# Two cached attention blocks on one core: the Q projection in matmuls of 320 columns instead of 160, with smaller first weight loads, no second warm-up and a new order table

## The chip, the cores and the metric

The kernel runs on one core of a Trainium2 chip. The metric is the device time of one execution in microseconds (us), as the median of three runs; lower is better. Before the change it is 734.2 us (runs 734.12, 734.2 and 735.46).

## The reference, cut to what matters

Two independent problems, A and B, with their own inputs; their outputs are put side by side. For each of them, with 16 batch rows (`B`), 80 query positions (`Sq`), model width 576 (`D`), 32 query heads, 16 key/value heads, 512 cached positions (`Sk`) and head width 128 (`Dh`), all in bfloat16:

```python
q = (x @ wq).reshape(B, Sq, 32, 128).transpose(0, 2, 1, 3)   # x: 16 x 80 x 576, wq: 576 x 4096
k = repeat(k_cache, 2, axis=1)                               # k_cache, v_cache: 16 x 16 x 512 x 128
v = repeat(v_cache, 2, axis=1)
scores = einsum("bhqd,bhkd->bhqk", q, k) * 128 ** -0.5
o = einsum("bhqk,bhkd->bhqd", softmax(scores), v)
out = o.transpose(0, 2, 1, 3).reshape(B, Sq, 4096) @ wo      # wo: 4096 x 576
```

## The kernel before

**Tiling.** The work is cut into 128 units. A unit is one batch row with four key/value heads, that is eight query heads, or 640 rows of scores against 512 cached positions. Eight units (eight batch rows, the same eight heads) make an octet; there are 16 octets, and two octets run interleaved, unit by unit. The constants are `NG` octets, `goct` the octet's number, `bl` the batch row inside it, and `U` the unit's number.

**One unit on TensorE (PE).** Scores come as four matmuls of 128 rows (`qk`, line 684) and one tile for the 32 rows that each head pair has left over (`qkr`, line 671, which packs four small matmuls into strips of the array, for two units at a time). VectorE (DVE) takes the negated row maximum (line 693), ScalarE (ACT) the exponential with its row sum (line 697), DVE the reciprocal (line 703), and GpSimd (POOL) scales the rows (line 706). Then PE transposes the probabilities in 40 small matmuls that use the two halves of the array's rows (`tr`, line 738), DVE or ACT copy them out of PSUM (lines 749 to 758), PE multiplies with V (`pv`, line 781), and DVE or ACT copy the result to `oT` (line 795). The output projection (`op`, line 830) adds 16 heads at a time.

**The Q projection.** For each octet there are eight sessions, `m` = 0 to 7. The contraction over 576 is done as four chunks of 128 rows and a tail of 64 rows. Before the change a session covers two batch rows (160 columns of `xT`) and four heads. Each of its two halves (`qp`, line 550) puts two heads side by side into one PSUM bank, eight matmuls of 160 columns. The tail (`qt`, line 565) adds four matmuls of 64 rows, two of which share the array because they use different row halves; outside the first two octets it is emitted at the head of a unit's `tr`. Two evictions of 320 columns (`qev`, lines 578 and 579) then scale the result and write it to `qT`. A session is tied to the unit `us` at whose `tr` its tail runs; sessions with `us` under 2 come ahead of the units.

**Loads.** All loads are issued on SyncE's queue (SP), in order. K comes through transposing DMAs, one for two units (`ldk`, line 637, 1 MB each, three pairs of buffers); V as one copy for each unit (`ldv`, line 641, 512 KB, six buffers); the Q weights `wq_sb` as one copy of 1 MB for octet pairs (`ldwa`, line 514), only that of the very first octet in four pieces of 256 columns; the tail rows `wt` in two copies of 64 KB (`ldwt`, line 518); x of problem A in blocks (`ldx`, line 387, two and then three blocks of 128 rows for each half of the batch rows); `wo_sb` in four copies for each half of the heads (`ldwo`, line 606).

**Start.** PE first runs eight matmuls on zeros (`warm`, line 348), later three more (`warm2`, line 363), and transposes x of problem A (`xtr` and `xt`, lines 408 and 426).

**What sets the order.** Every operation belongs to a stream with an order of its own (a sort key). A table of letters written out by hand, `ORDER`, then merges the streams: each letter takes the next operation of its stream, a quote mark ahead of it picks the other one of DVE and ACT, and digits behind it name the PSUM banks. Each engine runs its operations in the table's order, and the waits between engines are worked out from reads and writes. So the table fixes what stands behind what on each engine and on SP.

Of the kernel before, what the change touches and what calls it, by code (L numbers as in the profile page):

```python
# [13 lines left out]
LA = 11.5  # L14
# [14 lines left out]
NWARM2 = 3  # L29
NWC = 4  # L30
RG = ((0, 1, 2), (3, 4))
TS0 = 4.5
US0 = 2
QF = 12
LQ = 11
# [3 lines left out]
Q0K = ((-6.0, 1.0, 6.0, 11.0), (-4.6, 2.5, 8.0, 13.0))  # L39
# [13 lines left out]
WQ1 = -21  # L53
# [6 lines left out]
LETTERS = "abcdefghijklmnopqrstuvwxyzABCDEFGHIJKLMN"  # L60
ORDER = """
nEJni7GJIHIHMHj3k4Hj5LLHEHad3j7Md5j6k2LKdd4A'Bj6d3Ldj5A'Bd6d3dd4Bd1dd3A'B'AJKd0LaEdd4'A'Bd5e0e1odf2'Aod3lpe7d4
lodme0Ad6'Boe1ld3BJloe2hdhCe7old4uaoe0lvd5Cole1NudAf2ld7up'Be6ouj0md3Llodf02'ABd1'Bp'Ak3j4lpd5CmLdue7Be6md4ou'
Ae0CCd5loudKvlhAg1237oaN'Be4u'wj6x'zk5oe1ule2j7LuK'yolg0356LlCof47u'xz'yc1uclpj3vd5CLme2upc6e3'w'suoe4cmd1holF
g07CouFltc2av'ycxe6B'wd3u'zse0loc7d2olce1ltg46o'Ae0le7od5'zc1Colucc6scluxd0Ct'wv'yf17A'Budpe6'Be2ud3Cpme0uoc4m
cud1A'sholg57FCoFlue4zad6'yvolf27uwc5lpcd0A'x'tpe4mg35o'Bd2C'zyve1lwc5uocme3c4suc'Aoe5ld7te6loe4b1xo'Ble3Cobul
oub5lqhCluhe0e1hoe6ug34aolbCo'xu'yClue0qd3w'Bvd5'zAoulf17g24ulppmc6cc0scc1'tzc'xe6'sd0Cwumoc4e1u'ycod7'Avltc2e
3Bclhog46hCsalue1wc5o'xe2u'ycd3z'Bv'Ae4tle7d6Coub5oluoe0lbolc4'qcf12'slg57pCe4uy'xb0'wmBhuC'zhod5uhc7Alcavpe1e
6boutle4Coe3ud7mquc1olcg02vo'slCc6uyce1x'te4uzd0'wlod6'Be2olb3olc7Cue1lbou'Ach'qf25shlg34apCpc7u'zcb1C'wC'yuA'
xmve0e4od3muc2t'Bucold5vslf67ug02pub'wz'xmpc4'Be2q'ye6oe5h'Acd1holhd3Colug02lud6y'tv'we5'zxc4Bcmc2oe0e3'sCcoau  # L70
c7'tcAle4ue2oc1lcsd5olg07tob3'x'zy'wlBe1e0oblCoulc7he2e5uhocc4v'se1qclCd7uth'Ad3Coluf06olug24Cplub5'zumve1e4'x
oab'yu'wCpluc2comud0sc1'qe6le2ocd5'Atlg47o'BCf16uw'ze3lpub7'yCAvmoe2e0ve4ob'xluoc1uC'qcle3usd7aolc1ucp'Bd2log0
5tld4z'xe1'wB'yd3Cmoe0uc5oclug26slAIf15C'zxGue7'ye0hob6v'BIoluhe2Ce3plbuo'wumd7CAv'qe0oc4lcuoc6lcutc2clpe1e4oa
d3's'tog06ld2'wz'yd1xmBc6e0lAe3cCoue7'sg45Colvoc6'zuce0'ytd5uloe6ub4hlCoIule3e7uob'xa'wlvBCd0'AqulCf16ovg24plu
c3'yzuce7mwd2xuCo'sc4'Bce1'td3olg04AhlGe7'yc5Ccx'zvpb1wumoe0e4uobluole6uc7o'qcld0tc1A'Bf47'slcpe2'sd3Comug56pl
ue1xc4'zwaco'ye2d6t'Aloc5cc4lsce0Bd5mCove1g23tluof47u'zwAe0lb3pI'xo'Bhe1mbhCou'yhpe6hluc4oe2cld5Covle0d1saulqg
46ouCe2'wxub3'yBmuoe1lc4oblzclc7e0d6'qo'Ace1'sc3oe2lcd5t'tlog07f34w'zxe1'Ab7'yolCCe0ublouplc6ve1cmoad2uCd0Clqu
sc3'Bcug67'tuf15'zxupe3'yb7u'w'BAmvoc6ce0C'sd4uhole2hvbolhuhpld3qg06Cpuc7'wzu'xd2'yAc'Be0mhe6oc3c'td4ole1sc7lC
coug03htluCe6yd7'wv'x'zAe1d0umoc3uocle2Bc5'scole6hg34Ctlauof15'wvC'Axb2zlup'Bue7e6'yobumolc3qce0ld4oe1e2Csld6v
og37upub0xmBole6e5abzlo'wc7'yCcqu'Ae1oc3le0ud4old6ole2c'tc5sclCg17ou'thf03v'ywhAe5'xu'ze1ob4lCo'Bc7lcCpvd6se2m  # L80
uc5ocld7uhte0lug15oauCle2wbuo'zuyle0d5Ad1xCC'Boue2'qg67pulob4u'w'yzlue0bomCAle2uFc7ocFve6'sd3oFluf07FCqlve5pc4
'xcupd6'tmBc2cog14'slc2ye0'x'zcwe5oe1'Ad4moc3clCBd7vtlc6ouJe0e2'scoulg35tulof16'wC'zyd0u'ACe5xlue3Bc4cpud7h'sC
oe2umJb4Joulaoe1ulbolpg35lre2w'ze4Cyc1u'xb5ovAbluComue0rcld3uoe2'Bvd5loag46le0z'tc7'xe2'ywcoc6'se1k4olcd7o'Ac0
lBcCd3Kluf25'tvhCsg14DupDc6wuhcz'Ad0mupd4'xCymug27Buf15t'x'Bc3p'ye6caoc4mcsd2'twle1e4b3'zCo'Aue7oe0lvboluod6lr
g14lphe7z'yc3Dc'wohme0c4hb1olCAlue5xcoe2u'te7ad0'sCBule4obuolvc3Colce2urc6lcoue1e7sd5log34'tColuf26C'zvb1'x'wu
'yAe4lpue0d3oDubholvc7'Brcle4d5oamg01slb7y'z'wp'Ae0c4Come1ucbltuoe2d3loe0d4rDlohe1'xg67hCBluhof25'wDu'zAc0'yCc
pue7'sc3Cd6lxvoc'Buc0mthcd4Cuplg13u'suc7z'x'we0'ycvoe2'Be3ac1'Auoe4lcoc6lctd0Cmse7vd2olug15Ctluf36z'w'xu'yb4o'
AuBle0e1hod5hc7plce2Csbmvouod7lurg03lpDe1'ze4oc2'yce3x'thb0o'walAe2Blc5obolcCre1luc7oe4d3uold2Csclue0Cg15'toum
uf47'w'yb6vpGxumCDe1pbhvlAIoue4'zId3Blue0Cod5uCrg12luoDb6'xau'Blue5bmo'ze0c7'yod4lre1colc2e6cCslud5Co'tg07u'wl
Auf12w'yxue3p'ze6c0'BCchoumd7Ac5vlocd4vh'tplDg13use5zmc6e0oc'xac3'scwye2'td6loc3e1B'Acld5oc7olcg04Ct'suClf27ux  # L90
y'Be3u'ze1we5Job0uColvbpluAe4mc3ovd6rulcod2'shpe0lJg15ohe4zmIb3DC'xCoulac7e5ulcoe0bu'to'yvBle7d4ould2rle1Cwug0
5o'AuClf37xyuc6'wc'Bpc1'zve0scmue2oc6'Acte5G'sd3ColJd4oDle1hg06olhd2I'ywzac5'x'Ae0Cpclvc3d6t'Buome1cuoe5'sc4cu
log37tulCf04ulCwb1pv'x'yB'zue5k3moe6uc7boluKlce0d5'Aoc3re2lcCoe6ud1'so'tue0lg37hoDlCb2auwz'xlue6'ye7ob'A'Bpld3
oc5me0cold6rc4cse1'tg27olf45'ywhe0'zpb2hlCDxuoe7hbCvCloud1pmd0ur'ACle4ug23oa'Bule7xb6yumuc4'wcAuc5cBbvsoe0td4l
Crd5u'zoe1ug67olvf23Dw'zyhe0lc7xDcp'Bc6'se1oc'Ae7mhoc5cd4lCoud2'tsule0pc6cvlog15tle7xd6z'yae0'wo'Be1c5mcCouc2l
cCAd3u'sC'tf47oulg25pulb0vxmBuCw'ye1e3hoe4u'zbh'Aouloc6ue2ld5ovle1crc3lscDd4oe0lg26oa'tCCb1luxp'wue3'AbmouB'yu
e0Cd5'zoue2le7od4vlrg36ulohf01ylc2xc'wCzc3u'Ac'spe7v'the6c5'BoDcumb3Coulpe0uc4loe2e7abolC'sd6urld5vcug23tob4mz
lxe0boCle1uFre7d3o'wFu'Bd4'yCDAulf05FovDg26plFuc1'yxcCwuc7mBe2co'ze4d0'tA'sd6olg37plc2w'ye1xcC'Azvc3mcoe0ud4't
aole7c3od5lse1lcoe0c2'scolg37B'tf16y'wlb2Cxp'B'Ae0Cd3'zvohme5uc7ocle4ue1obluo'se0ulqc5ad7pulcoug24Ctlud1w'zue5
e0mob4xCo'Be6ub'youle2vqlc7hcAhc4lochd3s'te0lCug45ouCCf27'wx'zyud6'Aple5uc4oe1mcud0B'soulg23pvld4y'we5'zxe1oac  # L100
2'Acmd3Covc6ltcue7Blc2oc'sg05tlCf12z'x'w'ye7e6'Aob5Colvhe0c4h'Boculc7hpe3uchlbshuomd4uple0ud6og13Ctuqb7'zyulxw
e1Ce5moauc3ce0ovle2bAuloe1'Bod4lc6Coud5lscu'qe0Clg23ovtf17ulzb6u'xw'ype0e2moe3baolBd1loc5cqd0lsCg26'Aue5u'zxb3
o'wAlc4pe6d1'yhCoucmc5Bhcule2td7o'sf04lg56pCpe2u'ybxmovd5'wC'zuBc0qle7ucoe6'the3ud2'Aolg01Coulc7xu'wcy'zc6cA'B
c1mthe0cCaod5lue2'svc4lcd3utog67slf04Czu'ye1e2xb7ouovlbp'wlBe1c6Amchoe2c3'soe0lce6od5lCd1qulog27vpb0utmCwuCyle
3e4avbo'zuxod6'Blqe1d7o'Ae0lCg35olf24wxAd1'BClye7vc6oc'zuhc3'sce0u'thc6oe5lGb3uoIlupIe7buComuclqd0ule2e3ob5'so
lg67pe2xlbwCyv'zc3Cmouce7q'Bhc6ucloae0e5uo'Ad4'tud2olusg13lCuf67xlzuc0'ycpe5'Be3od1'w't'Ad2olpg04mCuc5y'xc'zhc
# [12 lines left out]
3umCoDue0'se6hod1ulc5pvlce2obv'taClug05ruob3'zuyle0e6'x'wbCmoule2vrc7co'Bd3'soDlc5e0DAcld7og46tlCvf12w'x'yBue0
'Ae5pd4'zuomd3uog67lplc1xcCw'yc0uze5mcoud6'tse7le2oae0c1'BcCAle5uc3od4'suolcvg17tlf23x'yoe0'zb1o'BlCwe7upd4lho  # L120
# [146 lines left out]
def bass_concat_heads__gqa_block_cached__gqa_block_cached__near_ridge_kernel(  # L267
# [27 lines left out]
    with ExitStack() as es:  # L295
# [55 lines left out]
        def em_warmend(e):  # L351
# [4 lines left out]
              name="warm", stream="W", alloc=[vw])  # L356
        S.add("dve", -980, em_warmend, reads=[R(vw, 0)], writes=[R(("warm",), 1)], name="warmend", stream="warmset")
        vw2 = S.bank()

        def em_warm2(e, vw=vw2):  # L360
            last = None
            for _ in range(NWARM2):
# [580 lines left out]
```

## Time and profile before

| what | value |
|---|---|
| median of three runs | 734.2 us |
| the profiled execution's own time | 733.71 us |
| its span, from the first to the last instruction | 732.0 us |
| granted TensorE clock over the span | 1.00 |
| PE busy | 719.2 us |
| ACT busy, DVE busy | 646.7 us, 639.3 us |
| moved by DMA | 160.90 MB, mean 220 GB/s |

Times in a timeline count from the span's start. The page names an engine, a line of the kernel, the tile written and the tiles read, the shape, the count, the busy time and the mean of one. A matmul's busy time overlaps that of the next one, since they are pipelined; what one costs in a row of them is therefore read from the distance between starts. "Idle before" is time in which the engine did nothing, with what ended it behind the arrow.

### The profile page before, as it was taken

Reading aid. Unit: us, or ns where it says so; the run is one execution under the profiler, and the core shown is the slowest. Engines: PE = TensorE matmul, PEld = TensorE weight load, DVE = VectorE, ACT = ScalarE, POOL = GpSimd, SP = SyncE. Lnnn points to the kernel's source line nnn. Section 1 sums busy time; section 2 is a strip of 40 time slices with the busy share of each in tenths; the row PEclk is TensorE's granted clock in tenths of the full one; section 3 lists DMA queues with packets and bytes.
Section 4 is the critical chain, followed back from the end, with each engine's and each line's share of the span. In section 5 each row is a group of like instructions: output and inputs, shape, how many; then the busy total and the mean of one; then the engine's idle time right before and its main releaser. Section 6 shows DMA issues by size and latency. Waiting matters only on the chain.

```text
span 732.0 us, 28848 instructions
## 1 busy us (share of the span) xinstructions
PE 719.2 (98%) x12103; PEld 565.2 (77%) x12103; DVE 639.3 (87%) x1457; ACT 646.7 (88%) x1847; POOL 433.9 (59%) x650
## 2 busy tenths in 40 slices
PE   7999999999999999999999999999999999999998
PEld 5677787777877777778777877787887878777677
DVE  2988888988899888899898998989889998889995
ACT  2998889999989899999898988899989989999993
POOL 0555557654766556566556565565755746647773
DMA  9999976988989899999989999899889998699951
GB/s 253 248 231 258 285 204 175 251 201 197 261 204 258 208 233 261 229 234 268 225 215 221 234 239 215 180 240 242 223 177 241 240 225 223 130 231 216 235 134 47
DMA packets 362354, 160.90 MB, mean 220 GB/s; under 512 B 274416, under 2 KB 358640, under 8 KB 362224
## 3 DMA queue, kind: packets, MB, share of 16 engines
q1 hardware_dynamic: 362224, 159.05, 92.7%
q8 instruction: 96, 1.57, 0.9%
q14 instruction: 34, 0.28, 0.1%
HBM read 87.65 MB, written 2.95 MB: 124 GB/s over the span
## 4 chain that ended last, share of the span: by engine, by line
PE 94%; DMA 2%; ACT 1%; DVE 1%; issue 1%; SPq 0%
PE ps L830 22%; PE ps L781 19%; PE ps L550 18%; PE ps L684 15%; PE ps L738 10%; PE ps L671 5%; PE ps L565 4%; DMA kT<-in_A_k_cache_dram 2%; DMA wt<-in_A_wq_dram 1%; ACT p_sb L697 1%; DVE negmax L693 0%; ACT qT L578 0%; DVE oT L795 0%; SPq L514 0%; ACT pT L749 0%
## 5 line engine op out<-in xcount | busy, mean ns | idle before, releaser
L706 POOL TENSOR_SCALAR p_sb<-p_sb,rinv 128x512 bf16<-128x512 bf16 x640 | 432.1, 698 | 280.2 <-DVE rinv L703 279.6
L697 ACT ACTIVATE p_sb<-ps,negmax 128x512 bf16<-128x512 f32 x640 | 442.0, 706 | 28.5 <-DVE negmax L693 21.4
L693 DVE TENSOR_REDUCE negmax<-ps 128x1 f32<-128x512 f32 x640 | 419.6, 680 | 37.2 <-PE ps L684 27.1
L781 PE MATMUL ps<-pT,v_sb 128*128 128x160 bf16 x2048 | 191.0, 233 | 2.2 <-ACT pT L756 1.2
L830 PE MATMUL ps<-wo_sb,oT 128*128 128x288 bf16 x1280 | 181.4, 286 | 0.0
L550 PE MATMUL ps<-xT,wq_sb 128*128 128x160 bf16 x2048 | 178.2, 233 | 1.7 <-DMA wq_sb<-in_A_wq_dram 1.6
L781 PEld LDWEIGHTS ps<-pT,v_sb 128*128 128x128 bf16 x2048 | 152.7, 98 | 34.2 <-issue 3.5
L684 PE MATMUL ps<-kT,qT 128*128 128x512 bf16 x512 | 177.2, 380 | 0.0
L550 PEld LDWEIGHTS ps<-xT,wq_sb 128*128 128x128 bf16 x2048 | 149.4, 98 | 22.8 <-issue 2.6
L830 PEld LDWEIGHTS ps<-wo_sb,oT 128*128 128x128 bf16 x1280 | 121.1, 98 | 44.4 <-ACT pT L756 2.5
L697 ACT ACTIVATION_READ_ACCUMULATOR p_sb<-ps,negmax 128x1 f32 x640 | 140.9, 220 | 0.0
L749 ACT COPY pT<-ps 128x512 f32<-128x512 f32 x165 | 96.5, 601 | 10.5 <-PE ps L738 9.8
L738 PE MATMUL ps<-ident,p_sb 64*128 64x64 bf16 x5120 | 96.1, 190 | 2.0 <-issue 0.7
L738 PEld LDWEIGHTS ps<-ident,p_sb 64*128 64x128 bf16 x5120 | 88.0, 95 | 4.9 <-issue 1.5
L578 ACT ACTIVATE qT<-ps 128x320 bf16<-128x320 f32 x140 | 62.0, 453 | 17.8 <-PE ps L565 14.2
L795 DVE CAST oT<-ps 128x320 bf16<-128x320 f32 x132 | 63.5, 481 | 9.5 <-PE ps L781 8.4
L751 DVE COPY pT<-ps 128x1024 bf16<-128x1024 bf16 x91 | 62.1, 682 | 9.9 <-PE ps L738 8.7
L795 ACT CAST oT<-ps 128x320 bf16<-128x320 f32 x124 | 53.9, 442 | 10.4 <-PE ps L781 9.5
L684 PEld LDWEIGHTS ps<-kT,qT 128*128 128x128 bf16 x512 | 47.9, 97 | 19.0 <-ACT p_sb L697 3.8
L579 DVE TENSOR_SCALAR qT<-ps 128x320 bf16<-128x320 f32 x116 | 55.3, 481 | 6.0 <-PE ps L565 2.6
L758 DVE COPY pT<-ps 128x256 bf16<-128x256 bf16 x133 | 36.4, 282 | 10.6 <-PE ps L738 8.2
L671 PE MATMUL ps<-kT,qT 128*32 128x512 bf16 x512 | 40.0, 384 | 2.2 <-DMA kT<-in_A_k_cache_dram 1.7
(33 smaller groups left out, 196.4 us busy)
## 6 DMA issues: line engine op xcount, KB each, us to landing
v_sb<-in_A_v_cache_dram SPq DMA_DIRECT2D x64, 512.0 KB, 5.3
v_sb<-in_B_v_cache_dram SPq DMA_DIRECT2D x64, 512.0 KB, 5.0
wo_sb<-in_A_wo_dram SPq DMA_DIRECT2D x8, 576.0 KB, 6.6
wo_sb<-in_B_wo_dram SPq DMA_DIRECT2D x8, 576.0 KB, 7.0
wq_sb<-in_B_wq_dram SPq DMA_DIRECT2D x4, 1024.0 KB, 6.0
wq_sb<-in_A_wq_dram SPq DMA_DIRECT2D x3, 1024.0 KB, 6.2
out_dram<-osb SPq DMA_DIRECT2D x40, 72.0 KB, 3.8
wq_sb<-in_A_wq_dram SPq DMA_DIRECT2D x4, 256.0 KB, 5.6
```

The lines of the kernel that those rows point to most:

```text
L550: last = e.matmul(ps[:, vbq[h].phys, QO + 160 * r:QO + 160 * r + 160], lhsT=wq_sb[:, wsl, ck, hi * 128:(hi + 1) * 128], rhs=xT[:, half, ck ...
L671: last = e.matmul(ps[32 * g4:32 * g4 + 32, vb_.phys, :], lhsT=qT[:, qsl_, bl_, g4 * 160 + 128:g4 * 160 + 160], rhs=k_of(U_, g4), start=Tru ...
L684: return e.matmul(ps[:, vb.phys, :], lhsT=qT[:, qsl, bl, gl * 160:gl * 160 + 128], rhs=k_of(U, gl), start=True, stop=True)
L693: return e.tensor_reduce(negmax[:, si:si + 1], ps[:, vb.phys, :], axis=AX.X, op=AluOpType.max, negate=True)
L697: return e.activation(p_sb[:, psl, :], ps[:, vb.phys, :], AF.Exp, bias=negmax[:, si:si + 1], scale=1.0, accum_out=rowsum[:, ss, k:k + 1])
L706: return e.tensor_scalar(p_sb[:, psl, :], p_sb[:, psl, :], rinv[:, ss, k:k + 1], 1.0, op0=AluOpType.mult, op1=AluOpType.mult)
L738: last = e.matmul(dst, lhsT=p_sb[64 * h:64 * h + 64, psls[k_], j * 128:(j + 1) * 128], rhs=ident[64 * h:64 * h + 64, 64 * h:64 * h + 64], ...
L749: return e.copy(pT[:, pts, :, :].bitcast(F32)[:, :, 32 * h:32 * h + 32], ps[:, vtp[h].phys, :].rearrange("p (n c) -> p n c", n=16))
L751: return e.tensor_copy(pT[:, pts, :, 64 * h:64 * h + 64], psb[:, vtp[h].phys, :].rearrange("p (n c) -> p n c", n=16))
L781: last = e.matmul(ps[:, vo.phys, off:off + 160], lhsT=v_sb[:, vs, gl, j * 128:(j + 1) * 128], rhs=pT[:, pts, 4 * gl + j, :], start=(j == 0 ...
L795: return (e.copy if en == "act" else e.tensor_copy)(dst, src)
L830: last = e.matmul(ps[:, vb.phys, 0:DC], lhsT=oT[:, hi, rb * 128:(rb + 1) * 128], rhs=wo_sb[:, wi, c3 * DC:(c3 + 1) * DC], start=(hi == 0), ...
```

## The change

A session now covers four batch rows (320 columns) and two heads, so that a half is one head: four matmuls of 320 columns in place of eight of 160, and two tail matmuls of 320 in place of four of 160. Session 0 to 3 of an octet make batch rows 0 to 3 for all heads, 4 to 7 the others. The eviction writes four runs of 80 columns instead of two by two. Since 320 columns need three blocks of x, x is loaded three blocks first and then two. The weights of the second octet are loaded in four pieces like those of the first, each on a semaphore of its own, and the tail weights are laid out in four groups of 128 columns, not two of 256. `LQ` goes from 11 to 12, so each session belongs to a unit one earlier, and the first one of the sessions that come ahead of the units is added to them. The second warm-up is gone. `ORDER` is new throughout, with PSUM banks and the choice of DVE or ACT.

```diff
-NWARM2 = 3
-QF = 12
-LQ = 11
+LQ = 12
-Q0K = ((-6.0, 1.0, 6.0, 11.0), (-4.6, 2.5, 8.0, 13.0))
+Q0A = -6.0
+Q0B = 1.3
-WQ1 = -21
+WQ1 = -28.0
+WQ1S = 0.3
+W4 = 2
...
-        wt = sb("wt", [128, 2, 2, 256], BF16)
+        wt = sb("wt", [128, 2, 4, 128], BF16)
...
-        S.add("pe", -LA - 13.2, em_warm2, reads=[R(("ones",), 0), R(("warm",), 1)], writes=[R(vw2, 0)],
-              name="warm2", stream="X", alloc=[vw2])
...
-        XP = ((0, 2), (2, 5))
+        XP = ((0, 3), (3, 5))
...
-            pieces = () if half else [(256 * i_, 256 * i_ + 256) for i_ in range(4)] if goct == 0 else ((0, 1024),)
+            pieces = () if half else [(256 * i_, 256 * i_ + 256) for i_ in range(4)] if goct < W4 else ((0, 1024),)
...
-                    src = wq_ap[512:D, q * 1024:(q + 1) * 1024].rearrange("p (a h c) -> h p a c", a=2, h=2)
+                    src = wq_ap[512:D, q * 1024:(q + 1) * 1024].rearrange("p (a h c) -> h p a c", a=4, h=2)
...
-                bp, hq = divmod(m, 2)
-                b0 = 2 * bp
+                bq, hp = divmod(m, 4)
+                b0 = 4 * bq
...
-                        for r in range(2):
-                            hi = 4 * hq + 2 * h + r
-                            for ck in range(4):
-                                last = e.matmul(ps[:, vbq[h].phys, QO + 160 * r:QO + 160 * r + 160],
-                                                lhsT=wq_sb[:, wsl, ck, hi * 128:(hi + 1) * 128],
-                                                rhs=xT[:, half, ck, n0:n0 + 160], start=(r == 0 and ck == 0), stop=False)
+                        hi = 2 * hp + h
+                        for ck in range(4):
+                            last = e.matmul(ps[:, vbq[h].phys, QO:QO + 320],
+                                            lhsT=wq_sb[:, wsl, ck, hi * 128:(hi + 1) * 128],
+                                            rhs=xT[:, half, ck, n0:n0 + 320], start=(ck == 0), stop=False)
...
-                    for r in range(2):
-                        for h in range(2):
-                            last = e.matmul(ps[:, vbq[h].phys, QO + 160 * r:QO + 160 * r + 160],
-                                            lhsT=wt[64 * h:64 * h + 64, wsl, hq, r * 128:(r + 1) * 128],
-                                            rhs=xT[64 * h:64 * h + 64, half, 4, n0:n0 + 160],
-                                            start=False, stop=(r == 1), tile_position=(64 * h, 0))
+                    for h in range(2):
+                        last = e.matmul(ps[:, vbq[h].phys, QO:QO + 320],
+                                        lhsT=wt[64 * h:64 * h + 64, wsl, hp, :],
+                                        rhs=xT[64 * h:64 * h + 64, half, 4, n0:n0 + 320],
+                                        start=False, stop=True, tile_position=(64 * h, 0))
...
-                        c_ = (4 * hq + 2 * h) * 80
-                        dst = qT[:, qsl, b0:b0 + 2, c_:c_ + 160].rearrange("p b (r s) -> p r b s", r=2)
-                        src = ps[:, vbq[h].phys, QO:QO + 320].rearrange("p (r b s) -> p r b s", r=2, b=2)
+                        c_ = (2 * hp + h) * 80
+                        dst = qT[:, qsl, b0:b0 + 4, c_:c_ + 80]
+                        src = ps[:, vbq[h].phys, QO:QO + 320].rearrange("p (b s) -> p b s", b=4)
```

The new table also sets a new order on SP. At the start it issues both parts of x, then all weights of the first two octets in eight pieces with their tail rows, then two K loads in a row; the four copies of `wo_sb` for the first half of the heads come ahead of the K load for units 8 and 9, where two of them came behind it. On PE all four sessions that make rows 0 to 3 of the first octet and the four of the second stand ahead of the first scores.

More of the change, by code (lines that the diff above doesn't have):

```diff
@@ L58 @@
 WOL = 1.2
-LETTERS = "abcdefghijklmnopqrstuvwxyzABCDEFGHIJKLMN"
+LETTERS = "abcdefghijklmnopqrstuvwxyzABCDEFGHIJKLMNO"
 ORDER = """
[L62 to L70, printed above, removed]
@@ L320, in bass_concat_heads__gqa_block_cached__gqa_block_cached__near_ridge_kernel @@
         sem_names = (["e_pe", "e_act", "e_dve", "e_pool", "d_x00", "d_x01", "d_x10", "d_x11", "d_wo",
-                      "d_wq0", "d_wq1", "d_wqs1", "d_wqs2", "d_wqs3", "d_wt0", "d_wt1", "d_xt"]
+                      "d_wq0", "d_wq1", *["d_wqs%d%d" % (i, j) for i in range(2) for j in range(1, 4)], "d_wt0", "d_wt1", "d_xt"]
                      + ["d_out%d" % i for i in range(NOSB)]
@@ L357, in bass_concat_heads__gqa_block_cached__gqa_block_cached__near_ridge_kernel @@
         S.add("dve", -980, em_warmend, reads=[R(vw, 0)], writes=[R(("warm",), 1)], name="warmend", stream="warmset")
[L358 to L362, printed above, removed]
-                last = e.matmul(ps[:, vw.phys, :], lhsT=ones, rhs=warm, start=True, stop=True)
-            return last
-        S.add("pe", -LA - 13.2, em_warm2, reads=[R(("ones",), 0), R(("warm",), 1)], writes=[R(vw2, 0)],
-              name="warm2", stream="X", alloc=[vw2])
-        S.add("dve", -LA - 13.1, em_warmend, reads=[R(vw2, 0)], writes=[R(("warm",), 2)], name="warmend",
-              stream="warmset")
         IDENT = R(("ident",), 0)
@@ L544, in bass_concat_heads__gqa_block_cached__gqa_block_cached__near_ridge_kernel, with em_qp @@
                 for h in range(2):
[L545 removed]
+                    def em_qp(e, h=h, hp=hp, wsl=wsl, half=half, n0=n0, vbq=vbq):
                         last = None
[L547 to L553 removed]
@@ L558, in bass_concat_heads__gqa_block_cached__gqa_block_cached__near_ridge_kernel, with em_qt @@
+                        return last
+                    S.add("pe", x + 0.001 * h, em_qp, reads=[R(("wq", wsl, hp), wv)] + xr,
+                          writes=[R(vbq[h], 0)] + [R(("qT", qsl, bl, 2 * hp + h), goct) for bl in range(b0, b0 + 4)],
                           name="qp%d.%d.%d" % (goct, m, h), stream="Q",
                           alloc=[vbq[h]])
-                def em_qt(e, hq=hq, wsl=wsl, half=half, n0=n0, vbq=vbq):
+                def em_qt(e, hp=hp, wsl=wsl, half=half, n0=n0, vbq=vbq):
@@ L579, in em_qev @@
                         return e.tensor_scalar(dst, src, SCALE, None, op0=AluOpType.mult)
-                    wr_ = [R(("qT", qsl, bl, 4 * hq + r), goct) for bl in (b0, b0 + 1) for r in (2 * h, 2 * h + 1)]
+                    wr_ = [R(("qT", qsl, bl, 2 * hp + h), goct) for bl in range(b0, b0 + 4)]
                     td["q"].append((em_qev, wr_))
@@ L607, in em_ldwo @@
                                            src.rearrange("(h p) n -> p h n", p=128))
-                    S.add("sp", x, em_ldwo, writes=[R(("wo", wos), ci)] + ([R(("warm",), 3), R(("ones",), 1)] if ci == 0 else []),
+                    S.add("sp", x, em_ldwo, writes=[R(("wo", wos), ci)] + ([R(("warm",), 2), R(("ones",), 1)] if ci == 0 else []),
                           dsem="d_wo", name="ldwo%d.%d.%d" % (prob, hh, wc), stream="wo")
```

145 lines of the change are left out of this document (75 added, 70 removed).

## The prediction

> **What bounds the kernel now.** I read the page's busy times and its chain first.
>
> ```profile
> PE 719.2 (98%) x12103; PEld 565.2 (77%) x12103; DVE 639.3 (87%) x1457; ACT 646.7 (88%) x1847; POOL 433.9 (59%) x650
> ...
> PE 94%; DMA 2%; ACT 1%; DVE 1%; issue 1%; SPq 0%
> ```
>
> PE is busy for 98% of the span and makes 94% of the chain that ended last. Since a busy PE need not be PE at its pace, the view of waits, for PE alone, comes next (who waited for whom, us in total, times, longest).
>
> ```profile
> PE ps L671 <- DMA kT<-in_A_k_cache_dram: 1.7, 1, 1.7
> PE ps L550 <- DMA wq_sb<-in_A_wq_dram: 1.6, 1, 1.6
> PE ps L348 <- DVE wo_sb L341: 1.2, 1, 1.2
> PE ps L781 <- ACT pT L756: 1.2, 1, 1.2
> PE ps L781 <- issue: 0.9, 1, 0.9
> PE ps L565 <- DMA wt<-in_A_wq_dram: 0.9, 1, 0.9
> ```
>
> There is nothing longer; with four smaller rows PE waits for some 10 us of 732. The timeline of PE shows what a matmul costs in a row of them (start, us, line, shape, count):
>
> ```profile
> 62.44 0.81 PE L684 MATMUL ps<-kT,qT 128*128 128x512 bf16 x3
> 63.19 0.31 PE L565 MATMUL ps<-xT,wt 64*128 64x160 bf16 x4
> 63.34 0.75 PE L738 MATMUL ps<-ident,p_sb 64*128 64x64 bf16 x40
> 64.02 1.15 PE L830 MATMUL ps<-wo_sb,oT 128*128 128x288 bf16 x8
> 65.00 0.38 PE L684 MATMUL ps<-kT,qT 128*128 128x512 bf16 x1
> 65.22 1.27 PE L550 MATMUL ps<-xT,wq_sb 128*128 128x160 bf16 x16
> 66.42 0.61 PE L671 MATMUL ps<-kT,qT 128*32 128x512 bf16 x8
> ```
>
> Read it by starts. The eight matmuls of 288 columns take 65.00 - 64.02 = 0.98 us, 122.5 ns each; the one of 512 takes 0.22 us; four tails take 0.15 us. The sixteen of 160 take 1.20 us: 15 at 69 ns, and 165 ns for the last, because PE passes there from the whole array to a part of it, which costs 96 ns more. From all starts in the trace the medians are 69.2 ns for 160 columns, 122.5 for 288 and 216 for 512: a straight line, about 2.5 ns and 0.417 ns a column. So a Q matmul is already paid nearly by its columns.
>
> **The ledger.** Adding, over all neighbours in PE's program of before, the usual distance of such a pair of lines gives 718.0 us. PE's last matmul starts at 729.1 us, so all its waits together are 11.1 us: 3.2 by the time the first weights are there, 0.6 in small ones up to 45 us, 1.8 at K for units 8 and 9 (53 us), 1.4 at 69 us and 4.1 later, 1.7 of it near 690 us. From there to the end of the span it is 2.9 us, and I leave that alone: both programs end with the same matmuls of lines 781 and 830.
>
> **The change part by part, on PE.**
> - Main matmuls: 1024 pairs of 160 become 1024 of 320. The line gives 135.8 ns for 320, against 2 x 69.2: 2.6 ns a pair, 2.7 us. The bounds are 138.4 (two of the old ones, no gain) and 133.3 (columns alone, a gain of 5.2 us); I take the line, since 288 is its near neighbour. In the new program the array is entered from whole to row halves 135 times, not 129, at 96 ns: 0.6 us back. Net -2.1.
> - Tails: four of 160 cost 4 + 77 + 4 + 66 = 151 ns; two of 320 share the array for 133 ns and 4, 137. That is 14 ns for each of 128, 1.8 us; the extra tail that stands by itself takes 0.3 back. Net -1.5; from nothing to -1.8.
> - Second warm-up: three matmuls of 512 at 216 ns, -0.65. They stood between two Q halves that had their weights, so PE was not idle there.
> - Order: with the same distances the rest of the new sequence comes to -0.65.
>
> The sum is -4.9, so PE's work is 713.1 us. That goes to the end wherever PE doesn't wait; the table by stretches shows where that is.
>
> ```profile
> 72.00:200.00 128.00, 127.52 (x2168) 101.07 (x2167) 110.60 (x249) 118.20 (x341) 76.96 (x116) 1.00 0.90 225
> 580.00:685.00 105.00, 104.43 (x1789) 81.74 (x1781) 95.52 (x217) 97.49 (x280) 66.64 (x100) 1.00 0.93 216
> ```
>
> Columns are the stretch, its length, then PE, PEld, DVE, ACT and POOL busy. ACT is next at 92 to 93%: 0.7% less time for it is no bound yet. The evictions stay 320 columns each (453 ns on ACT, 481 on DVE) and as many. Writing four runs instead of two by two I cost at nothing; the 320-column copy to `oT` that already writes four runs of 80 takes 442 and 481. That covers a gain or loss of up to 11 ns on ACT, under 2 us in 140 evictions, and ACT's idle time in the middle hides it.
>
> **What happens to the waits.** Here the queue of SP counts.
>
> ```profile
> 1.30 0.45 SPq L514 DMA_DIRECT2D wq_sb<-in_A_wq_dram  x1
> ...
> 5.81 2.19 SPq L514 DMA_DIRECT2D wq_sb<-in_A_wq_dram  x3
> 8.04 6.11 SPq L637 DMA_TRANSPOSE kT<-in_A_k_cache_dram  x1
> ```
>
> - First weights. Before, 1 MB had to land ahead of the first Q matmul (issued at 1.30, landed at 6.49, PE at 6.63). Now 720 KB of x and a piece of 256 KB go first. Two x blocks landed at 3.58, and the next MB took 2.9 us, so 0.69 MB more lands at about 5.7; DVE's third copy of xT (0.4 us each from 4.7) ends near 5.9. PE starts Q there with waits of 2.0 in place of 3.0. The other seven pieces land some 0.9 us apart, as the three did at 10.92, 11.83 and 12.72, and a session takes 1.41, so PE finds them there.
> - K. Three more issues at 0.73 us stand ahead of the first K load: issue at 10.4, landing 9.6 us later as before (17.68), at 20.0. PE's program reaches the first scores after 16.8 us of work, 18.8 with waits. So it waits 1.2 us. Everything on ACT and DVE starts 2.3 us later; on PE it costs only this wait, since two more sessions are done by then.
> - Up to 70 us. K for units 6 and 7 lands near 42 (40.89 before). Then come `wo`, `wo`, V, `wo`, `wo`, V and K for units 8 and 9. From K to the third copy took 6.8 us before, so V for unit 3 lands at 46.5 to 48.8, and PE wants it at 43.7 + 3.3 = 47.0: nothing to 1.8, I take 1.0. K for units 8 and 9 lands at about 58; in the new program it is wanted after 54.4 us of work (47.6 before), at 58.7, because the output projection and its `wo`, due at 51.7 and wanted at 52.5, now come ahead. So the wait of 1.8 goes, and half of the 1.4 at 69 us with it.
> - Later: 4.1 as before. The distances in PE work from a K load's release to its use are 11.7 us at least, 10.9 before, and the median is 17.5 after 16.9. One copy of tail weights for octet 12 has 7.0 us from release to use, while 64 KB take 5 to 6.2: up to 2 us may go there.
>
> Waits after: 1.2 + 0.8 + 1.2 + 0.5 + 1.0 + 0.5 + 4.1 = 9.3, or 6 to 13 with each at its ends. So -1.8.
>
> 733.7 - 4.9 - 1.8 = 727.0 for a profiled execution; the median lies 0.5 above the profiled one before, so **727.5**.
>
> **The rivals.**
> - *Early loads late.* If copies behind a K load come as slowly as the one that took 3.9 us (V at 44.81), V for unit 3 costs 3 us, the K behind it 1 more; waits of 14: 732. For it: in the stretch up to 53 us DMA is never at rest. Against it: K came 5 us apart later. With 2 us more at the tail weights it is 734, no change.
> - *The softmax engines set the pace* (slower). If ACT and DVE limit and not PE, nothing that PE saves counts, and the 2.3 us by which the first maximum (18.22) moves goes to the end: 733.7 + 2.3 + 0.5 = 736.5. It decides if ACT's idle time from 53 to 685 us (632 less 575 busy, 57 us) is used up in stalls. For it: ACT has no gap from 20 to 53 us. Against it: PE loses 3 us from 72 to 705.
> - *Fewer waits.* The new order loses only 6 us: 724.
> - *A matmul is paid by its weights.* If the 69 ns were the weight load's, 1024 loads less would save 71 us on PE; ACT (646.7 busy, 19.0 before its first exponential, 12.5 behind its last) would bound at 678. The line through 288 and 512 speaks against it. [...]
>
> **How the numbers follow.** Forecast 0.62; early loads late at 732, 0.14, and at 734, 0.06; softmax engines 0.08; fewer waits 0.09; weights 0.01. About 0.2% (1.5 us) is what a measurement of this kernel can tell from no change, so faster means under 732.7: 0.62 + 0.14 + 0.09 + 0.01 = 0.86; same 0.06; slower 0.08. The range from 724 to 732.5 takes in the pitch's bounds (2.7 either way) and the waits up to 14; it leaves out the softmax case, the 734, the weights and the better half of fewer waits, 0.2 in all.
>
> **What would show it.** Starts of Q matmuls 135 to 137 ns apart, and 0.14 us from a tail to its transposes; the first scores at about 20 us; no wait of PE for K at units 8 and 9, but one of about 1 us at V for unit 3. PE's waits should come to 9 us. A pitch over 138 ns, PE waits over 14 us, or waits of PE for ACT all along would make it wrong.

## The result, and the profile after

The kernel after the change takes **730.67 us** (median of five runs, 728.3 to 731.59) against 734.2. The ratio is 0.9938, with a 95% interval from 0.9916 to 0.9961. In three of the five executions, the profiled one among them, the mean granted clock was 0.997 or 0.998; they took 730.67 to 731.59, and the two at 1.000 took 728.3 and 728.83. The forecast was 727.5, so the sign and the range held and the size was 3.2 us too good.

The profiled execution took 731.59 us, 2.1 less than the one of before. First its page: the span, the busy times, the chain that ended last, the instruction queues and the group of the new Q matmuls.

```profile
span 729.8 us, 26289 instructions
...
PE 719.5 (99%) x10820; PEld 514.5 (71%) x10820; DVE 637.6 (87%) x1447; ACT 643.9 (88%) x1856; POOL 432.0 (59%) x650
...
q8 instruction: 86, 1.41, 0.8%
...
PE 87%; DMA 4%; ACT 3%; DVE 3%; SPq 1%; issue 1%; POOL 1%
...
L538 PE MATMUL ps<-xT,wq_sb 128*128 128x320 bf16 x1024 | 174.0, 299 | 0.3 <-DVE xT L402 0.3
```

PE has 1283 matmuls less and is as busy as before (719.5 and 719.2 us), so its busy time doesn't show the pace. The row q8 matters later: by their number its packets are PE's instructions, 256 in each. PE has 21985 of them here (weight loads, matmuls and a few semaphore instructions) to 86 packets, and in before 24549 to 96; 86 and 96 times 256 are 22016 and 24576. Then the view of PE's waits.

```profile
PE ps L767 <- issue: 1.9, 1, 1.9
PE ps L349 <- DVE wo_sb L342: 1.2, 1, 1.2
PE ps L724 <- DVE oT L781: 0.6, 1, 0.6
PE ps L657 <- DMA kT<-in_B_k_cache_dram: 0.5, 1, 0.5
```

The waits for weights and for K at units 8 and 9 are gone. At the top stands one that the prediction didn't have, and it has no releaser: "issue" means that the engine waited for nothing that the profile shows. PE's timeline shows the place (start, us, line, shape, count, idle time before).

```profile
193.58 0.61 PE L657 MATMUL ps<-kT,qT 128*32 128x512 bf16 x8
194.13 0.59 PE L767 MATMUL ps<-pT,v_sb 128*128 128x160 bf16 x6
196.60 0.30 PE L767 MATMUL ps<-pT,v_sb 128*128 128x160 bf16 x2 [1.89 <-issue]
196.74 0.38 PE L670 MATMUL ps<-kT,qT 128*128 128x512 bf16 x1
196.96 1.21 PE L767 MATMUL ps<-pT,v_sb 128*128 128x160 bf16 x8
197.96 0.63 PE L670 MATMUL ps<-kT,qT 128*128 128x512 bf16 x1
198.39 2.13 PE L816 MATMUL ps<-wo_sb,oT 128*128 128x288 bf16 x8
```

Eight matmuls with V are one operation, with waits only ahead of the first; PE stops between the sixth and the seventh, 2.05 us longer than usual. Behind it the eight of 288 columns take 1.92 us to the start of the next operation (at 200.31), where they took 0.98 before. The table by stretches says why (length, PE, PEld, DVE, ACT and POOL busy, granted clock):

```profile
190.00:197.00 7.00, 5.12 (x94) 3.64 (x87) 5.38 (x13) 4.51 (x16) 5.32 (x9) 1.00 1.14 241
197.00:200.50 3.50, 3.50 (x19) 2.47 (x18) 1.38 (x2) 2.93 (x8) 0.98 (x2) 0.51 0.72 186
200.50:210.00 9.50, 9.50 (x116) 6.88 (x113) 8.52 (x18) 7.20 (x21) 1.36 (x2) 1.00 0.59 119
```

For 3.41 us, from 197.0 to 200.4, the granted clock was 0.5, which cost 1.65 us more. It fell 0.4 us after PE had gone on at 196.60; why, the profile doesn't say.

### The profile page after: what moved, and what is told of

The parts are those of the page before. It is cut to its first block, busy times and chain, and to the rows that moved or that the text cites. A ratio compares the mean times of both kernels' runs of the same rounds, so it can differ in the third digit from the quotient of the medians.

```text
span 729.8 us, 26289 instructions
## 1 busy us (share of the span) xinstructions
PE 719.5 (99%) x10820; PEld 514.5 (71%) x10820; DVE 637.6 (87%) x1447; ACT 643.9 (88%) x1856; POOL 432.0 (59%) x650
## 2 busy tenths in 40 slices
DMA packets 365976, 160.73 MB, mean 220 GB/s; under 512 B 278560, under 2 KB 362784, under 8 KB 365856
## 3 DMA queue, kind: packets, MB, share of 16 engines
q8 instruction: 86, 1.41, 0.8%
## 4 chain that ended last, share of the span: by engine, by line
PE 87%; DMA 4%; ACT 3%; DVE 3%; SPq 1%; issue 1%; POOL 1%
PE ps L816 21%; PE ps L767 18%; PE ps L538 16%; PE ps L670 14%; PE ps L724 9%; PE ps L657 4%; PE ps L551 4%; DMA kT<-in_A_k_cache_dram 3%; ACT p_sb L683 3%; DVE negmax L679 2%; DMA kT<-in_B_k_cache_dram 1%; POOL p_sb L692 1%; SPq L503 1%; SPq L507 0%; ACT pT L735 0%
## 5 line engine op out<-in xcount | busy, mean ns | idle before, releaser
L767 PE MATMUL ps<-pT,v_sb 128*128 128x160 bf16 x2048 | 187.9, 233 | 2.3 <-issue 1.9
L538 PE MATMUL ps<-xT,wq_sb 128*128 128x320 bf16 x1024 | 174.0, 299 | 0.3 <-DVE xT L402 0.3
L538 PEld LDWEIGHTS ps<-xT,wq_sb 128*128 128x128 bf16 x1024 | 95.2, 98 | 44.3 <-ACT qT L564 1.6
L724 PEld LDWEIGHTS ps<-ident,p_sb 64*128 64x128 bf16 x5120 | 91.4, 95 | 9.3 <-ACT oT L781 1.9
L735 ACT COPY pT<-ps 128x512 f32<-128x512 f32 x145 | 85.2, 600 | 12.2 <-PE ps L724 11.9
L737 DVE COPY pT<-ps 128x1024 bf16<-128x1024 bf16 x111 | 75.7, 685 | 12.0 <-PE ps L724 10.6
L564 ACT ACTIVATE qT<-ps 128x320 bf16<-128x320 f32 x156 | 69.0, 454 | 17.8 <-PE ps L551 15.5
L565 DVE TENSOR_SCALAR qT<-ps 128x320 bf16<-128x320 f32 x100 | 47.2, 480 | 6.1 <-PE ps L551 4.5
```

Source lines behind the costliest of these rows:

```text
L538: last = e.matmul(ps[:, vbq[h].phys, QO:QO + 320], lhsT=wq_sb[:, wsl, ck, hi * 128:(hi + 1) * 128], rhs=xT[:, half, ck, n0:n0 + 320], star ...
L564: return e.activation(dst, src, AF.Identity, scale=SCALE)
L724: last = e.matmul(dst, lhsT=p_sb[64 * h:64 * h + 64, psls[k_], j * 128:(j + 1) * 128], rhs=ident[64 * h:64 * h + 64, 64 * h:64 * h + 64], ...
L735: return e.copy(pT[:, pts, :, :].bitcast(F32)[:, :, 32 * h:32 * h + 32], ps[:, vtp[h].phys, :].rearrange("p (n c) -> p n c", n=16))
L737: return e.tensor_copy(pT[:, pts, :, 64 * h:64 * h + 64], psb[:, vtp[h].phys, :].rearrange("p (n c) -> p n c", n=16))
L767: last = e.matmul(ps[:, vo.phys, off:off + 160], lhsT=v_sb[:, vs, gl, j * 128:(j + 1) * 128], rhs=pT[:, pts, 4 * gl + j, :], start=(j == 0 ...
```

## The experiments

Nearly all were read in one way beside their times. All versions of after run the same matmuls in the same order, except those of the Q projection and the warm-up. Matching the others one by one between two profiles gives the difference of their starts as a curve: a step in it is a wait that only one of the two has, a slope is a difference in what each matmul costs. All ratios are against the kernel before, run beside them (medians of 734.04, 734.36 and 734.14 us in the three groups; a ratio isn't exactly the quotient of two medians).

**again**: the kernel after, unchanged.

> The changed kernel once more. In its first profile PE stands still for 1.9 us inside one group of line 767 at 194.5 us, and the granted clock is 0.5 from 197.1 to 200.5 us. Theory A (the stall is a late fetch of PE's instructions, and the half clock follows from it by chance of phase): executions fall into two groups, at clock 1.00 near 728.5 us and at 0.997 to 0.998 near 731 us; the stall sits at the same instruction whenever it appears. Theory B (the half clock belongs to the start without the second warm-up): half-clock time appears within the first 20 us. Theory C (the chip was disturbed once): all executions at 1.00 and 728.5 us.

728.76 us, ratio 0.9939 (0.9917 to 0.996), clock 1.000 in all six executions. The stop is at the same instruction, and now without half clock behind it:

```profile
193.97 0.59 PE L767 MATMUL ps<-pT,v_sb 128*128 128x160 bf16 x6
195.89 0.30 PE L767 MATMUL ps<-pT,v_sb 128*128 128x160 bf16 x2 [1.33 <-issue]
```

So the stop belongs to the program, the half clock to the execution. Counted in PE's instructions (weight loads, matmuls and the few semaphore instructions), the stop is ahead of number 5569, which is 193 behind a multiple of 256. In before the stops inside an operation or a row of like ones are at 68.84, 151.48, 589.94 and 687.70 us, with a small one of 0.43 us at 286.33, at numbers 193 to 195 behind a multiple of 256 too. A block of 256 instructions is one packet of q8; why a block ends at 193 of this count and not at 0, the profile doesn't say. Below, a block whose first instruction PE had to wait for is called late.

**shift**: the first warm-up in small matmuls. The same columns, 112 PE instructions more, so that every later block begins at another operation.

```diff
-            for _ in range(NWARM):
-                last = e.matmul(ps[:, vw.phys, :], lhsT=ones, rhs=warm, start=True, stop=True)
+            for _ in range(8 * NWARM):
+                last = e.matmul(ps[:, vw.phys, 0:64], lhsT=ones, rhs=warm[:, 0:64], start=True, stop=True)
```

> The first warm-up is 64 matmuls of 64 columns in place of 8 of 512, the same columns in 112 more PE instructions; what follows is the same. In all profiles so far the stalls of PE inside a group sit at PE instruction 193 to 195 modulo 256. Theory A (fetch of instructions in blocks of 256): stalls inside groups are again at 193 to 195 modulo 256 of the shifted count, so not at the operations where they were; the one at 194.5 us moves or goes. Rival (the stall belongs to that operation, a wait that the records do not show): it stays at the same group of line 767.

726.15 us, ratio 0.9904 (0.9883 to 0.9926). No operation of PE is interrupted any more. The same place, from PE's timeline:

```profile
193.38 0.62 PE L657 MATMUL ps<-kT,qT 128*32 128x512 bf16 x8
193.93 0.73 PE L767 MATMUL ps<-pT,v_sb 128*128 128x160 bf16 x8
194.49 0.38 PE L670 MATMUL ps<-kT,qT 128*128 128x512 bf16 x1
```

Up to 193 us the profiled execution of after is 0.2 us behind it; then come the stop (2.05) and the half clock (1.65), and four steps of about half a microsecond by 693 us; at the end it is 6.0 behind. Not every step is a late block: the one of 0.6 at 606 us is a wait for a K load, which lands at 606.10. The same wait is 1.0 us in shift128 and oneload and 1.7 in split, and again and shift don't have it.

**shift128**: 32 warm-up matmuls of 128 columns, 48 instructions more.

```diff
+            for _ in range(4 * NWARM):
+                last = e.matmul(ps[:, vw.phys, 0:128], lhsT=ones, rhs=warm[:, 0:128], start=True, stop=True)
```

> After with its first warm-up as 32 matmuls of 128 columns (48 more PE instructions instead of 112, the same columns). Fetch theory: stalls inside groups, if there are any, are at PE instructions 193 to 195 modulo 256, so at other operations than in after (PE instruction 5569, at 194.3 us, isn't the same matmul any more); the time lies between 726.1, with none, and 729, with as much as after. Rival, that the shorter matmuls at the start gave the 2.6 us by themselves (clock or start): the same 726.1 and no stall at all.

726.51 us, ratio 0.9888 (0.9865 to 0.991). One stop of 0.74 us, at number 10945, which is 193 behind a multiple of 256, and at another operation than in after. The time doesn't tell the two theories apart, but the place of the stop speaks for the blocks' ends and against the small matmuls by themselves.

**halfv**: PE's program as in after, less traffic.

```diff
+                if U >= 6:
+                    return e.dma_start(v_sb[:, vs, :, 0:256], src[:, :, 0:256])
```

> After, with PE's instructions unchanged, but from the seventh unit on each V copy loads only half of its bytes (256 of 512 columns, into buffers that hold old data in the other half), so that the loads move about 32 MB less of 159. This leaves out part of the input. Theory: the stalls inside groups at PE instructions 193 to 195 modulo 256 (5569 at 194 us above all) come from fetch packets that queue behind the loads; with less traffic they go, and it takes what the version with 64 small warm-up matmuls took, 726.2. Rival, that a block boundary costs this whatever the DMA does: the stall at 5569 stays and it takes 729.

725.98 us, ratio 0.9884 (0.9859 to 0.9908). Of the stop at number 5569 some 0.3 us is left, and that is the largest:

```profile
194.10 0.59 PE L769 MATMUL ps<-pT,v_sb 128*128 128x160 bf16 x6
194.86 0.30 PE L769 MATMUL ps<-pT,v_sb 128*128 128x160 bf16 x2 [0.17 <-issue]
```

So it is neither the program nor the block's end alone. Four versions stop ahead of this same instruction, and the records of q8 show the packet of its block in each (times in us):

| run | packet starts | PE instructions still to go | packet ends | PE goes on | longer than usual |
|---|---|---|---|---|---|
| after | 194.20 | 10 | 195.32 | 196.60 | 2.05 |
| again | 193.29 | 31 | 194.34 | 195.89 | 1.50 |
| oneload | 192.74 | 86 | 193.74 | 195.06 | 0.75 |
| halfv | 192.40 | 119 | 193.50 | 194.86 | 0.33 |

The packet itself takes 1.0 to 1.1 us in all four, and the median of the 86 in after is 1.07. **The block comes late because its packet starts late**; the median packet of after starts 186 instructions ahead. Over the fourteen profiles the first instruction of a late block starts 1.1 to 1.6 us after its packet has ended. Where PE got there 2 us after that or later, it never stopped inside an operation. That halfv, with less traffic (128.75 MB against 160.73), has the earliest start and its other blocks in time points to the loads; how a packet is queued among them isn't shown by the trace.

**shiftbefore**: before with the 64 small warm-up matmuls (the edit of shift).

> The kernel before, with its first warm-up cut into 64 matmuls of 64 columns (the same columns, 112 more PE instructions), as in the run with 64 small warm-up matmuls of after, which took 726.15. Fetch theory: the four stalls inside groups of before (1.46, 0.67, 0.90 and 1.15 us from start to start, at PE instructions 193 to 195 modulo 256) move to other places and mostly go, so about 3 us come off 734.04: 731; any that stay are at 193 to 195 modulo 256 again. The change itself is then worth 731 - 726.2 = 5 us. Rival, that the pauses belong to the work there (ACT at 69 us): they stay at the same operations and it takes 734.

729.46 us, ratio 0.9934 (0.9911 to 0.9957): this edit alone gives before 4.9 us, about what the change gave. The stop at 69 us is gone, and so is the wait of 1.8 us for K of units 8 and 9, which is no block's end, though nothing on SP was changed. There are new stops of 1.2, 0.5 and 0.5 us, at 193 to 195 again. From here to shift it is 3.3 us by the medians and 4.4 by the profiled spans (728.2 and 723.8), and these stops are about 2.1 of it.

**oneload**: the second octet's weights as one load of 1 MB (and its three letters less in the table).

```diff
-            ... if goct < W4 else ((0, 1024),)
+            ... if goct == 0 else ((0, 1024),)
```

> The weights of the second octet come as one load of 1 MB again; three issues fewer stand ahead of the first K load. Theory A (the later first K costs PE a wait of 0.4 us and lets ACT and DVE start late, which PE pays with 1.8 us of waits from 30 to 47 us): the first scores move from 18.9 to about 17.7 us, waits up to 47 us fall by 1 us or more, 727.5 us at full clock. Rival (DMA bytes and not issues set the start of K): K lands when it did, no change. Rival (the 1 MB load makes PE wait for weights): 1 to 2 us slower.

727.45 us, ratio 0.9924 (0.99 to 0.9947). K lands at 17.70 us, not 18.89, and the first scores start at 18.61 without a wait, not at the 17.7 expected: PE has Q matmuls to do until then. Matched with **again**, PE is only 0.16 us ahead from 20 to 190 us, so this is all that the earlier K gave there. The stop at number 5569 was 0.75 us shorter too, with its packet starting at 192.74 and not at 193.29.

**shiftone**: shift and oneload together.

> After with the 64 small warm-up matmuls (726.15) and, added to it, the weights of the second octet in one load (727.45 against 728.76 by itself). If the earlier K load gave that 1.3 us: 724.9. If 0.75 us of it was a shorter fetch stall at 194 us, which isn't there with the small warm-up: 725.6.

727.31 us, ratio 0.9901 (0.988 to 0.9922): no gain over shift; both expectations failed. The first scores start at 19.32 against 18.73, behind a wait for the second octet's weights that ends at 13.59, and one block is late (0.5 us at 457 us). So here the four pieces are worth at least what the later K costs.

**split**: each Q matmul of 320 columns as two of 160, the rest as after.

```diff
+                        for c_ in (0, 160):
+                            for ck in range(4):
+                                last = e.matmul(ps[:, vbq[h].phys, QO + c_:QO + c_ + 160], ...
+                                                rhs=xT[:, half, ck, n0 + c_:n0 + c_ + 160], ...
```

> Each main Q matmul of 320 columns is issued as two of 160 with the same weights and the same table; all else is as in the changed kernel. Theory A (a matmul is paid by its columns and about 2.5 ns): starts 69 ns apart, PE's work 1024 x 2.5 ns = 2.6 us more, 731 us in executions at full clock, a third of the gain given back. Rival (the width brings nothing, the gain is all order and loads): within 0.5 us of the changed kernel. Rival (it is paid by its weight load): back at 734 us or slower.

730.33 us, ratio 0.9952 (0.9932 to 0.9971), and its stops moved with the 2048 instructions added (1024 matmuls, each with its weight load). The price is in the curve: from 200 to 500 us, without a step, the starts fall 0.95 us behind those of shift, in which 432 Q matmuls run there. That is 2.2 ns each, 2.25 us for 1024.

**shiftsplit**: split with the 64 small warm-up matmuls.

> After with the 64 small warm-up matmuls (726.15) and each Q matmul of 320 columns split in two of 160. Pitch theory: 1024 times 2.6 ns, 2.7 us more: 728.8, whatever the fetches do if no stall is inside a group. Rival, that the width is worth only what the split gave without the small warm-up (1.6 us): 727.7. If a matmul were paid by its weights, some 70 us more.

735.3 us (733.02 to 738.52 in 12 runs), ratio 1.0013 (0.9996 to 1.0031). Both expectations failed, by 6.5 and 7.6 us, and yet the slope of the curve from 200 to 500 us is the same 0.95, once two steps at block ends are taken out. The rest are other steps: 1.2 at the first scores, 0.7 at 547 us, and this one, ahead of number 6338, 194 behind a multiple of 256:

```profile
195.06 0.74 PE L726 MATMUL ps<-ident,p_sb 64*128 64x64 bf16 x39
197.80 0.20 PE L726 MATMUL ps<-ident,p_sb 64*128 64x64 bf16 x1 [2.00 <-issue]
```

The other executions lost more than the profiled one, 733.02, and the profile can't say where.

**shifttail**: shift, with each tail as four matmuls of 160.

```diff
+                    for c_ in (0, 160):
+                        for h in range(2):
+                            last = e.matmul(ps[:, vbq[h].phys, QO + c_:QO + c_ + 160], ...
```

> After with the 64 small warm-up matmuls, and each tail as four matmuls of 160 columns again instead of two of 320. By the prediction's term (14 ns for each of 128) PE ends 1.8 us later, 727.9; by the distances measured in after (147 ns for two against 151 for four) 0.5 us, 726.7. Fetch stalls come on top where a boundary is late and are read off by matching the starts.

731.51 us, ratio 0.9962 (0.9943 to 0.9981); both expectations failed. Nearly all of the difference from shift is in late blocks: steps of 1.3, 2.1, 0.8 and 0.6 us. The slope from 200 to 500 us is 0.13 us for 54 tails, 2.4 ns a tail, 0.3 us for 128.

**shiftwarm2**: shift, with the second warm-up put back behind the first Q half.

> After with the 64 small warm-up matmuls, and the second warm-up of three matmuls of 512 columns put back behind the first Q half. The prediction's term is 0.65 us; by it PE's matmuls are 0.65 us later from there on, 726.8. Rival, that waits for the first weights and for K hide it: PE is less than 0.3 us later at the first scores, 726.2.

726.15 us, ratio 0.9886 (0.9855 to 0.9916). At 25 us PE is 0.1 later than in shift, at the end too: waits at the start hide the rest of the 0.65.

**twoexp**: shift, with two exponentials more on ACT at 25 us.

```diff
+                    if U == 1 and k in (1, 2):
+                        e.activation(xs[:, 7 + k, 640:1152], ps[:, vb.phys, :], AF.Exp, bias=negmax[:, si:si + 1], scale=1.0)
```

> After with the 64 small warm-up matmuls, and two more exponentials of 128x512 on ACT behind those of two tiles of unit 1 (written to unused memory, without a row sum: about 0.57 us each, 1.15 in all, at 25 us). If ACT sets PE's pace from 30 to 47 us, PE's matmuls behind 47 us start 1.15 us later than without them, and the time is 727.3. If ACT has slack there and the 1.8 us of small waits is something else: less than 0.4 us, 726.3.

729.46 us, ratio 0.9924 (0.9897 to 0.9951). The same operation of PE, first in shift, then here:

```profile
38.43 0.62 PE L657 MATMUL ps<-kT,qT 128*32 128x512 bf16 x8
...
39.69 0.62 PE L657 MATMUL ps<-kT,qT 128*32 128x512 bf16 x8
```

From 30 to 50 us PE is 1.25 later than in shift, 0.13 of it from before the added work, so 1.1 of ACT's 1.15 arrive at PE at once: ACT does set its pace there. Of the other 2.7 us of the profiled execution 2.1 are late blocks (at 54, 63 and 70 us), in a program of PE that is the same as in shift, so that its blocks end at the same instructions; 0.4 is a wait ahead of an operation at 516 us.

## Why the prediction was right in sign and too good in size

The prediction's ledger against PE's last matmul in the profiled execution, which starts at 726.9 us:

- **Main matmuls.** Forecast 2.7 us gained, 0.6 back. The median distance is 136 ns (135.8 forecast), and whole to row halves costs 96 ns as before. Taken out alone the width is worth 2.25 us. About right. The lines of after, with a tail behind:

```profile
50.86 1.25 PE L538 MATMUL ps<-xT,wq_sb 128*128 128x320 bf16 x8
52.05 0.31 PE L551 MATMUL ps<-xT,wt 64*128 64x320 bf16 x2
52.19 0.75 PE L724 MATMUL ps<-ident,p_sb 64*128 64x64 bf16 x40
```

  By starts the eight take 1.19 us, seven at 136 ns and 232 for the last, ahead of the row halves.
- **Tails, mis-sized.** Forecast -1.5. Two of 320 take 146 ns to the start of the transposes, not 137. Of the four of 160 the first pair took 79 ns and the second 69; the prediction gave the pair of 320 only its columns and 4 ns, as for a second pair, but it pays the 10 ns of a first pair too. By shifttail it is 0.3 in place of 1.8, so about nothing with the lone tail. This term cost the forecast 1.3 to 1.5 us.
- **Second warm-up, mis-sized.** Forecast -0.65, 0.1 where it was tried. The reason given, that PE was not idle there, overlooked that PE waits for something else soon behind it, so that of the time saved some 0.55 us has gone into waits by 25 us. The order's -0.65 was not tried by itself.
- **Start.** PE's first Q matmul starts at 6.58, and the first scores wait 0.4 us, as the timeline says:

```profile
6.58 0.72 PE L538 MATMUL ps<-xT,wq_sb 128*128 128x320 bf16 x4 [0.30 <-DVE xT L402]
...
18.94 1.04 PE L670 MATMUL ps<-kT,qT 128*128 128x512 bf16 x4 [0.31 <-DMA kT<-in_A_k_cache_dram]
```

  The first weights landed at 6.39 (5.7 forecast), K at 18.89 (20.0 forecast). Waits took 1.4 us ahead of the first Q matmul, the last of them for DVE's copy of `xT`, and 0.4 for K; 0.8 and 1.2 were forecast, so the sum was about right. The ledger's "usual distance" of one pair that occurs once, from the last transpose of x to the first tail, also held a wait of 0.95 us (1.10 us from start to start in before, where a transpose and the way into the row halves take 0.15), in both kernels' work; that is most of the 1.1 us by which PE is ahead of the forecast at 29 us.
- **29 to 53 us, the wrong place.** No wait for V of unit 3: it landed at 46.06, ahead of the 46.5 to 48.8. But PE loses some 2.5 us in small waits (1.5 forecast for this stretch), where ACT is full. From the table by stretches of after (PE, PEld, DVE, ACT, POOL):

```profile
30.00:36.00 6.00, 5.95 (x107) 3.83 (x99) 5.71 (x15) 5.77 (x17) 3.57 (x6) 1.00 1.11 223
36.00:42.00 6.00, 5.42 (x51) 3.18 (x53) 5.87 (x14) 6.00 (x20) 2.66 (x4) 1.00 1.17 281
42.00:48.00 6.00, 5.75 (x120) 3.44 (x117) 5.10 (x13) 5.97 (x19) 6.00 (x11) 1.00 1.09 382
```

  The step that failed is "on PE it costs only this wait, since two more sessions are done by then": with more done, PE is through sooner and meets ACT, and twoexp shows that there 1.1 of 1.15 us more on ACT are PE's. It is the softmax rival for 20 us, not for the whole kernel.
- **K of units 8 and 9.** The wait went, as forecast. The operation that reads this K, in before, in shiftbefore and in after:

```profile
53.14 0.61 PE L671 MATMUL ps<-kT,qT 128*32 128x512 bf16 x8 [1.72 <-DMA kT<-in_A_k_cache_dram]
...
51.32 0.61 PE L671 MATMUL ps<-kT,qT 128*32 128x512 bf16 x8
...
59.14 0.61 PE L657 MATMUL ps<-kT,qT 128*32 128x512 bf16 x8
```

  K landed at 53.00, 49.01 and 55.40 us. So the new order does make room, 3.7 us of it (landing at 58 and use at 58.7 forecast). But with the old order and the same loads K came 4 us sooner in shiftbefore, and the wait was gone there as well: that before waited at all hung on how its loads ran, and that the order is what removed the wait is not shown.
- **69 us.** The 1.4 us that the view gave to ACT in before was a late instruction block: its packet starts at 67.80 and ends at 68.80, 1.4 us ahead of PE's next instruction at 70.20. The lines of before, and behind them the same matmuls in shiftbefore:

```profile
67.80 1.28 PE L781 MATMUL ps<-pT,v_sb 128*128 128x160 bf16 x16
70.31 0.71 PE L781 MATMUL ps<-pT,v_sb 128*128 128x160 bf16 x8 [1.23 <-ACT pT L756]
...
65.99 1.83 PE L781 MATMUL ps<-pT,v_sb 128*128 128x160 bf16 x24
```

  The gap comes at a block's end (number 1987, 195 behind a multiple of 256) and goes in shiftbefore. ACT's copy starts 1.64 us behind the first of these matmuls in both, and in shiftbefore PE doesn't wait for it: the view named the wrong releaser. In after nothing is left of it (0.5 forecast).
- **Later.** Forecast 4.1. Without the stop at 194 us and the half clock it is 4.0, some 0.9 us of it in two other late blocks (546 and 693 us) and 0.6 in the wait for K at 606 us; of before's 4.1 late blocks were 2.6, or 3.1 with the small one at 286 us. **The 2.05 and 1.65 us at 194 to 200 us are what the forecast lacked**: no row of the page priced them.

The balance from 727.0 forecast for a profiled execution to 731.6: late block 2.05, half clock 1.65, tails 1.3, ACT from 29 us 1.0, less 1.1 from the start and 0.5 at 69 us, makes 4.4 of the 4.6. So what the change itself does to PE's work is, as an estimate, about 2.4 us (1.6 width, 0.1 warm-up, 0.65 order, as far as that holds), half of the 4.9; between shiftbefore and shift 2.3 are left when the stops are taken out. Between the profiled executions of before (733.71) and of again (729.05, full clock) lie 4.7 us: about 2.4 of work, 1.8 of the wait for K and some 2 less in late blocks (4.5 against 2.4), with about 1.5 more lost where ACT is full. The late blocks (4.5 us in before, 2.4 in again, none inside an operation in shift, 0.33 for the largest in halfv) differ with PE's program and with the loads, and in shiftbefore the wait for K went with an edit of the first warm-up alone. So the work that the prediction was about is worth half of what it said, and that the time still fell into its range is **partly luck, on both sides**: in the profiled execution the stop and the half clock took 3.7 us, while the wait for K (1.8) and late blocks of before that have gone (4.5 against 0.9 in the others here) gave more than that back.

Of the rivals, early loads late (732) came nearest in size for the profiled execution, but by another mechanism: the loads came in time. That a matmul is paid by its weights is out: 1024 loads less saved 2.25 us, not 71.

The best versions that were run are shift, shift128, shiftwarm2 and, with half of most V loads left out, halfv: 726 us, and their intervals can't tell them apart. In the first three few blocks are late (shift has no stop inside an operation, shift128 one of 0.74 us, and shiftwarm2 ends 0.1 us behind shift), but shiftsplit, shifttail and twoexp have the same small warm-up as shift and lost 2 us and more in late blocks.

## What to carry to other kernels

When PE stops inside an operation, where nothing is waited for, count its instructions: here the stops 193 to 195 behind a multiple of 256 came with packets of instructions that started late (10 to 119 PE instructions ahead in the four versions above, against a median of 186 in after), and edits that added PE instructions or changed a load shuffled them by 0.75 us (oneload against again) to 4.9 us (shiftbefore against before, with a wait for K in it). So a gain below 1% is to be judged by matched starts (slopes and steps), and a forecast of it needs a term, and a range, for that shuffle. PE's time saved ahead of a stretch in which ACT is full was lost there in waits (of 1.15 us put on ACT in twoexp 1.1 reached PE): before costing a delay at nothing, look whether ACT has a gap behind it.

## What the runs showed of the hardware

- PE's instructions came in packets of 256 on the queue q8 (21985 to 86 packets of together 1.41 MB in after, 24549 to 96 in before), and where a packet started and so ended late, PE stopped for 0.3 to 2.2 us at the instruction 193 to 195 behind a multiple of 256, with no releaser, or a wrong one, in the view of waits. At most blocks PE didn't stop; in before it stopped for 0.4 us or more at five of the 96, and these took 4 to 4.5 us.
- A stop of 2.05 us was followed by a granted clock of 0.5 for 3.41 us in the profile of after; in three others with stops of 2.1 to 2.2 us (shifttail, shiftsplit) or 1.5 (again) the mean clock was 1.000. What decides between them was not tried, and it stays open, as does the spread of shiftsplit.
- Two matmuls that share the array by row halves took about 10 ns more than one matmul of as many columns in a row (in after 146 against 136 ns for 320, in before 79 against 69 for 160), but a second pair right behind a first of 160 took 69: the 10 ns were paid once.
